# A two-layer memory-augmented transformer on one core: P times V as one 128-row product per head, V in 64-column tiles, and a new order of TensorE's work

## The chip, the cores and the metric

The kernel runs on one core of one Trainium2 chip. Its time is the device time of one execution in microseconds (us). Three runs of the kernel before took 2775.19, 2775.85 and 2778.07 us, so the median is 2775.85 us. The profile below is of one more execution, whose span is 2772.4 us.

## What is computed

The input has 2048 rows of width 576. Attention (A) and a gated feed-forward net (B) follow each other, and the pair is applied twice with the same weights:

```python
x = x + A(layernorm(x));  x = x + B(layernorm(x))
x = x + A(layernorm(x));  x = x + B(layernorm(x))

# A: 64 segments of 32 rows, one after the other; 32 heads of 128
for s in range(64):
    h = concat([mem, xs[s]])                 # 8 memory rows + 32 rows = 40 tokens
    q, k, v = h @ Wq, h @ Wk, h @ Wv         # 576 -> 32 x 128 each
    p = softmax(mask(q @ k.T * 128**-0.5))   # 40 x 40 for each head
    o = (p @ v) @ Wo                         # 32 x 128 -> 576
    mem, out[s] = o[:8], o[8:]               # the next segment reads mem
# B: out = (silu(x @ w1) * (x @ w3)) @ w2, inner width 4608
```

A segment needs the memory rows that the segment before it made, so each layer is a chain of 64 steps. The kernel runs the two layers together: step t works on segment t of the first layer and on segment t-7 of the second (a lag of seven). There are 71 steps, t = 0 to 70. In steps 7 to 64 two segments go through every product together, as 80 columns ("double steps", 58 of them); the first seven and the last six steps have one segment, 40 columns ("single steps").

## The kernel before

576 is four chunks of 128 and a remainder of 64. Each product is therefore a node of 128-row matmuls and a small node for the remainder of 64 rows, with two remainders side by side in the upper and the lower half of the array. The program is made of such nodes. Each node of TensorE has a letter and a tiling of the array, which the planner calls its mode:

| letter | node | tile (rows x columns) |
|---|---|---|
| Q, q | Q and K of four heads; remainder | 128x128; 64x128 |
| S | scores | 128x64 |
| T, P | transpose of the probabilities; P times V | 128x128; 64x128 |
| O, o | output product; remainder | 128x128; 128x64 |
| X, x | V of segment rows; remainder | 128x32; 64x32 |
| V, v | V of memory rows (and the segment rows next to them); remainder | 128x32; 64x32 |
| F, f, W | feed-forward up, its remainder, down | 128x128; 64x128; 128x128 |
| m, a, b, p, n | small transposes | 128x128 |

The planner takes the order of these nodes from a string, `ORDER = FIRST + FOUR * 11 + LAST`; FOUR is a stretch of four steps that stands eleven times. From it, and from model times, it assigns copies out of PSUM to ScalarE or VectorE ("AD" nodes). The parts that the change touches:

```python
def v_nodes(name, t, prio, tail_at, emit, users, deps, tail_deps):
    sl = Slot("v", users=users)              # one of 4 buffers of V
    b = banks()                              # two PSUM banks
    m_ = node("PE", ..., mode="c32", acq=[sl] + b, name=name)
    n = node("PE", ..., deps=[m_] + tail_deps, mode="oct", name=name + "t")
    ev = [node("AD", ew(512), em.v_ev(sl, r, b[r]), deps=[n], ...) for r in (0, 1)]

def v_mm(self, t, b, strips, tail):          # four strips of 32 columns
    for c in ((4,) if tail else range(4)):
        for r in (0, 1):
            for p0, c0, q in strips:
                out = self.bk(b[r])[p0:p0 + 32, :]
                ...                          # HTt[:, c, c0:c0+32] x W[:, c, 512 columns]

def v_ev(self, v, r, b):
    return lambda n: self.cp(n, self.T.V[:, v.i, r, :], self.bk(b)[:])

def pv(self, t, g, pts, vx, vm, b):          # eight heads
    todo = [(0, s) for s in vx] + [(1, vm)]
    for hl in range(4):
        for m, s in todo:
            for ab in (0, 1):
                rr = slice(ab * R64, (ab + 1) * R64)
                self.mm(bank[ab][...], self.T.V[rr, s.i, ...], PT[rr, m, hl, :],
                        m == todo[0][0], m == 1, tile_position=(ab * R64, 0))

def step(t):
    for k in ((0, 1) if e else (0,)):        # e = role(t): 1 in even steps
        ... v_nodes("VM", ...)
    for g in range(NG):                      # four groups of eight heads
        ...                                  # Q q Q q, S, softmax, T, copies to PTS, P, copies to OT, O, o

def load_qk(self, kind):                     # all of Wq, then all of Wk, then both remainders
    for c in range(4):
        self.dma(self.T.W[:, 4 * kind + c, :], wd[c * P:(c + 1) * P, :])
    if kind:
        for r, wd in ((0, self.a.wq), (1, self.a.wk)):
            self.dma(self.T.W[r * R64:(r + 1) * R64, 8, :], wd[4 * P:D, :])   # 64 partitions
```

In the last function the remainder of Wq lies in partitions 0 to 63 and that of Wk in 64 to 127. The remainder of Wv is loaded as two such halves. The pool `pts` has one buffer: a T has to wait until the P before it has read it.

Of the kernel before, what the change touches and what calls it, by code (L numbers as in the profile page):

```python
# [13 lines left out]
P = 128  # L14
R64 = 64
# [16 lines left out]
SWITCH = 0.1  # L32
# [3 lines left out]
POOLS = {"bank": 7, "y": 1, "qkt": 4, "v": 4, "sme": 2, "pb": 2, "pts": 1, "ot": 2,  # L36
         "xr": 4, "xn": 2, "w13": 2, "w2": 2, "htt": 4}
# [7 lines left out]
class Slot:  # L45


    def __init__(self, pool, users=1):
        self.pool, self.users, self.i, self.end = pool, users, None, 0.0


class Node:
# [11 lines left out]
    def after(self, *more):  # L64
        for d in more:
# [7 lines left out]
         "WO": "O", "WOt": "o", "VX": "X", "VXt": "x", "VM": "V", "VMt": "v", "FF": "F", "FFt": "f", "W2": "W"}  # L73


def plan(nodes, pools, letters):
# [24 lines left out]
    def est(e, n):  # L101
        t = max(t_eng[e], n.ready)
        need = {}
        for s in n.acq:
            need[s.pool] = need.get(s.pool, 0) + 1
        for p, c in need.items():
            t = max(t, sorted(free[p])[c - 1])
        return t
# [4 lines left out]
    while len(order) < len(nodes):  # L113
# [32 lines left out]
        for s in n.acq:  # L146
            f = free[s.pool]
            s.i = min((i for i in range(len(f)) if f[i] <= st + 1e-9), key=lambda i: f[i])
            f[s.i] = NOW
# [32 lines left out]
def ewh(*ns):  # L182
# [5 lines left out]
    "maQQqqSQQqQQqSQqqTqSQVvVqPvTOPSToOPXOToPoxOoQQqqQQSqqQSqVQqvQSTqPQTqPSTOoPOOToPoaOoQQqqQQqqSVSvQQqqQTSqQqPVSTOPv"  # L188
    "oTXPOToPOOooxQQqqQQSqqQqSQQqVSqQqvTSPTOPoTOPoTOPoOoQQpqqVQvqSQnQqqFQqfSTFfPSQQqqWFTOPfSoFOfVvTWFPfoXTFPOOoofxQqQ"
    "QqqQFSqfVSvQWQqqQTqSQPqFfOTFfPSoTWPOFofOTFPfoOoWQQqqFQfqVvWFQqfSFQSfqVvWQFqfQSqTFfPQOTqWFPfSoTFPfOOWToPoOoabQQqq"  # L190
    "QQqqSVSvQQqqXxTSXxPQTQqqOSPToPOOToPoOoQQpqqQQSqqQQqqSVVvvTnQPqSFTQPfqOFSofXTOoPxWTFFfPfOOooWQQqqFfQFSfqQQqqVSvQT"
    "QqqFQPfSqFWSfXTFfPxOTOWooPFTFffPOOooWQFqfQqQFafqQWFSqfQQqqSFWQqfVVSvvFfTQqPWFSfTFfPOToWPOoTOPoOboQQqqQpQSqqQXxSQ"
    "qqVSvQqTQPqXTSPxOTOoPoTPOOoonQQpqqQQSqqVnQqSvQQqqFTfFPfQOTqSoFWVvSfPFTWOPfXTOFxofPFOWooWQfqQQqqQFfqSVvWFWQTqfSQX"
    "xqFWQqPfSWQTOqPFoSfOTFPfoWFTWOPfFOooWQfqQQqQqqSWQFfqSVvFTQqWQqfWaQqPFSSfTFVvfPOWWFTfoOPoTWPOOoobQQqqQQSqqQQSqqVX"
    "TvSxQqPQTqOoSPXxTOPopTWPOOoon"
)
FOUR = (
    "QQqqQpQSqqVVvvQTQqqPSnQFQSqqfOTFPfSoXxTFfPFWWOFToffPOOooWWFQfqQQqqQFqfSFWWQfqXVxvSQTWQqqFPfSTWQFPfqOOToSoWFPfFTO"
    "PfWOooFQfqQQqqWWFQqfVSSvQQqqWFTQqfPSWFQfqVvSTWWFFPffOoTOPoTWPOoOoabWQQqqQQSqqQQqqVSSvXxTQqPQqTOPSXxoTOPopTOPoOon"
)  # L200
LAST = (
    "QQqqQpQqqSVvSQnQqqQTqQFqPfSSFTOPfVvFTOoofPFWWTOPfoFOfoWQWFqfQQqqWFWQSfqVXxvQSqXxQqTFQqPfSQFfqOTFWPfoSWOTFfPFTOoo"
    "fPWOWoFQqfFWWQqfFQSfqQVvqQWQSqqWTFQfqQSPqWFTOSoPfVWFvfTOPoTWPOOoobQqpQQqqQSqQqSXVvxQTqQSPqQTqXPSOxoOTWPToPOOoonQ"
    "QqqpQSqVQnvqQTSqPFQfqFQTOqfPSFQOqfVoSovWWTFfPFTOPfWOFWooXxQqfVQqvQQSqqWQqSFTQqfFWQQqSqPfTFSPfOWTOooWPFTFfPfOOooW"
    "WQFfqQqFQQqfqSWFWQqfSVvFQfqWWSFQqfTFfPQqWTWOFSoPfVvTOWoPTWPOObooQQpqqQQSqqQQqqSnXVvxFfSTQqPQFTqfOoSPFTOoPfWTOPFO"
    "fooFQqfQqVSQvQqqWQTFfqFSPfVQqvWTQFSfqFQPqfOOoSoWTFfPXxTFPfWOOooFQfqQqQQSqqQSVqvWQTFfqQSPqFfQqTOSoPWOTFPfoTFfPOOo"
    "oWQqFQfqQQSqqVvSQQqqQTQqqSPTSVPFvOToOPoTfOoPOopWnFFffFfFWfFFffWFfWFfFfFWfFfFWfFFffWFfFfWFfFfWW"
# [4 lines left out]
class Opt:  # L212

    qk, qkt, sc, tr, pv, wo, wog, vm = 0.0079, -0.0342, 0.0268, 0.1447, 0.0406, 0.2653, 0.0725, 0.1407
    vmt, vx, vxt, ff, fft, win, w2, gstep = -0.0231, 0.2313, 0.0843, 0.2124, -0.1839, 2.4, 0.1943, 0.0624
# [3 lines left out]
def make_nodes(em, nseg, pools, o=Opt, dma_bw=230e3, load_bw=380e3):  # L219
# [26 lines left out]
    ld_m0 = load("m0", kb(8, D), -10, em.load_m0())  # L246
    ld_qk = [load("ldqk", kb(576, 4096), kd - 9.0, em.load_qk(kd)) for kd in (0, 1)]
    ld_v = [load("ldv", kb(576, 4096), -7.0, em.load_v())]
# [44 lines left out]
    vx_slots, vx_nodes, vx_pe, last_v = {}, {}, [None], [None]  # L293

    def v_nodes(name, t, prio, tail_at, emit, users, deps, tail_deps):
        sl = Slot("v", users=users)
        b = banks()
        m_ = node("PE", 8 * 0.2165, emit(b, False), deps=deps, prio=prio, mode="c32", acq=[sl] + b, name=name)
        n = node("PE", 0.2165, emit(b, True), deps=[m_] + tail_deps, prio=prio + tail_at, mode="oct", name=name + "t")
        reads_ht.setdefault(t, []).extend([m_, n])  # L300
        ev = [node("AD", ew(512), em.v_ev(sl, r, b[r]), deps=[n], prio=prio, rel=[b[r]], name=name + "e") for r in (0, 1)]
        return sl, ev, n

    def vx_pair(t, prio):

        deps = [ht_ready[li, s] for s in (t, t + 1) for li in layers_of(s) if s == t or li]
        for k in ((0, 1) if both(t) else (0,)):
            sl, ev, vx_pe[0] = v_nodes("VX", t, prio + 0.01 * k, o.vxt, (lambda k: lambda b, tail: em.vx(t, k, b, tail))(k), 4,
                                       deps + vx_pe + last_v, [])
            for kk in ((k,) if both(t) else (0, 1)):  # L310
                vx_slots[t, kk], vx_nodes[t, kk] = sl, ev

    def step(t):
# [9 lines left out]
        vm_slots, vm_nodes = {}, {}  # L323
        for k in ((0, 1) if e else (0,)):
            pv_ = t + o.vm + 0.01 * k
            sl, ev, last_v[0] = v_nodes("VM", t, pv_, o.vmt, (lambda k: lambda b, tail: em.vm(t, k, b, tail))(k), 2 if e else 4,
                                     hm[:1] + hx + (ld_v if t == 0 else []), hm[1:])
            for kk in ((k,) if e else (0, 1)):
                vm_slots[kk], vm_nodes[kk] = sl, ev
        me = steps[t]  # L330
        if t == nst - 1:
            last_reads[0].append(last_v[0])
        y = Slot("y", users=2)
        wos, wots = [], []
        for g in range(NG):
            k = g // 2
            qs, qe = [], []
            for u in (2 * g, 2 * g + 1):
# [3 lines left out]
                m_ = node("PE", 32 * mm80, em.qk(t, u, b), deps=hx + hm[:1] + (ld_qk if t == 0 else []),  # L342
                          prio=pq, mode="full", acq=[q] + b, name="QK")
                n = node("PE", 4 * mm80, em.qk_tail(t, u, b), deps=[m_] + hm[1:], prio=pq + o.qkt, mode="row", name="QKt")
                rd += [m_, n]
                me[f"QK{u}"], me[f"QKt{u}"] = m_, n
                for kind in (0, 1):
                    qe.append(node("AD", ew(256, 64) if nl == 2 else ew(160), em.qk_ev(t, u, kind, q, b[kind]), deps=[n], prio=t + o.ustep * u,
                                   rel=[b[kind]], name="QKe"))
# [10 lines left out]
            w = 0.168 * (4 if nl == 2 else 2 - e) + nl * 320 / 960  # L360
# [8 lines left out]
            x_slots = [] if nl == 1 and e else [vx_slots[t - e, k]]  # L369
            x_nodes = [] if nl == 1 and e else vx_nodes[t - e, k]  # L370
            pv = node("PE", (8 if x_slots else 4) * mm80, em.pv(t, g, pts, x_slots, vm_slots[k], b), deps=pe_ + vm_nodes[k] + x_nodes,
                      prio=pf + o.pv, mode="row", acq=b + [ot], rel=[pts, vm_slots[k]] + x_slots, name="PV")
# [11 lines left out]
        if t == nst - 1:  # L384
            last_reads[1].extend(me[f"QKt{u}"] for u in range(8))
# [21 lines left out]
    last_up = [None]  # L407
# [3 lines left out]
    def job(j):  # L411
# [10 lines left out]
        prev_ff = last_up[0]  # L422
        cost = ewh(640)
        for (bi, g) in reversed(ents):
            pa = post(bi, g)
            wr += ln_nodes("F", xr[g], Slot("xn"), [pa], s0, [((lambda bi: lambda b: em.xtb_write(bi, b))(bi), cost, [prev_ff])], last)
# [14 lines left out]
        for at, pp in enumerate([npp - 1] + list(range(npp - 1)) if last else range(npp)):  # L441
            mids, w2s, htts, lds = [], [], [], []
            stays = last and pp == npp - 1
            for pr_ in (2 * pp, 2 * pp + 1):
# [8 lines left out]
                else:  # L453
                    keep = s0 < nst <= s0 + 4 and pp == npp - 1
                    w13, w2 = Slot("w13", users=1 + keep), Slot("w2", users=ne + keep)
# [8 lines left out]
                          acq=b + [htt], name="FF")  # L464
                ff = node("PE", 2 * mm, em.ffn_up(ents, pr_, w13, b, last and not stays, True), deps=[fm], prio=prio + o.fft, mode="row",
                          rel=rel13, name="FFt")
                a = node("ACT", actc(256 * ne), em.ffn_tanh(ents, b, htt), deps=[ff], prio=prio - 0.5, name="tanh")
                c = node("DVE", 2 * dve(256 * ne) + 0.13, em.ffn_mul(ents, b, htt), deps=[a], prio=prio - 0.5, rel=b, name="mul")
                last_up[0] = ff
                mids.append(c)  # L470
                htts.append(htt)
            for (bi, g) in ents:
                b = banks()
                d = node("PE", 8 * 0.1225, em.ffn_down(bi, pp, htts, w2s, b, last and not stays), deps=mids + lds, prio=prio + o.w2,
                         mode="full", acq=b, rel=htts + w2s, name="W2")
# [11 lines left out]
    def x_in(g):  # L487
        xn = Slot("xn")
        ld = node("DMA", 0.8, em.load_xn(g, xn), deps=reads_ht.get(4 * g - 3, [])[:1], prio=4 * g - 3.0 if g else -11, acq=[xn],
# [12 lines left out]
    for t in range(nst):  # L502
# [4 lines left out]
        if role(t) == 0:  # L507
            vx_pair(t, t - 1 + o.vx)
# [19 lines left out]
class Emitter:  # L528
# [28 lines left out]

    def swdma(self, out, in_):
        self.ch("POOL", self.nc.gpsimd.dma_start(out=out, in_=in_))
# [6 lines left out]


# [27 lines left out]
    def load_m0(self):  # L595
        return lambda n: self.dma(self.T.M0[0:MEM, :], self.a.mem0[0])

    def load_qk(self, kind):
        def f(n):
            wd = (self.a.wq, self.a.wk)[kind]  # L600
            for c in range(4):
                self.dma(self.T.W[:, 4 * kind + c, :], wd[c * P:(c + 1) * P, :])
            if kind:
# [628 lines left out]
```

## Time and profile before

| | busy, us | share of the span |
|---|---|---|
| TensorE matmuls (PE) | 2723.5 | 98% |
| TensorE weight loads (PEld) | 2252.7 | 81% |
| VectorE (DVE) | 2047.1 | 74% |
| ScalarE (ACT) | 1091.0 | 39% |
| GpSimd (POOL) | 328.4 | 12% |

A record of a matmul covers its whole way through the array, some 180 to 200 ns for 80 columns, while matmuls of one kind start every 36 ns. Busy time of PE therefore overlaps itself, and the distance from one start to the next tells more. The trace has 60919 matmuls. Every one of them can be assigned to its letter, since the number of matmuls of each node is fixed by the code.

### The profile page before, as it was taken

What the parts mean: (1) busy time and instruction counts of PE and PEld (TensorE: products, weight loads), DVE (VectorE), ACT (ScalarE), POOL (GpSimd) and SP (SyncE); (2) the same over time, 40 slices, a digit from 0 to 9 for tenths busy, and PEclk for the clock granted to TensorE, in tenths of its full rate; (3) what the DMA queues carried; (4) which work ended last, traced back from release to release, by engine and by line L of the source; (5) the groups of instructions that cost most, each with busy time, mean ns of one, the idle gap of its engine ahead of it and who ended that gap; (6) DMA issues with size and microseconds to landing.
All of it is one profiled execution on the core that took longest, in us unless ns stands there. A gap on an engine that the chain in (4) does not pass through costs nothing.

```text
span 2772.4 us, 136269 instructions
## 1 busy us (share of the span) xinstructions
PE 2723.5 (98%) x60919; PEld 2252.7 (81%) x60919; DVE 2047.1 (74%) x5584; ACT 1091.0 (39%) x3339; POOL 328.4 (12%) x399
## 2 busy tenths in 40 slices
PE   5999999999999999999999999999999999999999
PEld 4887888888888888888888888888888888878887
DVE  4677777777777777777777777777777777687776
ACT  1434343433434343343434334343433434343332
POOL 1111010110101011010101101010101101010110
PEclk9999999999999999999999999999999999999999
DMA  8062614244242424424152342415234241523467
GB/s 308 13 198 69 184 53 138 81 121 124 78 131 62 140 82 116 128 78 131 56 146 82 112 133 77 131 49 153 82 106 138 73 130 57 142 79 107 141 182 235
DMA packets 481691, 322.02 MB, mean 116 GB/s; under 512 B 26216, under 2 KB 476656, under 8 KB 479440
## 3 DMA queue, kind: packets, MB, share of 16 engines
q1 hardware_dynamic: 478080, 306.38, 37.7%
q8 instruction: 476, 7.80, 1.2%
q0 software_dynamic: 3024, 6.93, 0.9%
q14 instruction: 111, 0.91, 0.1%
HBM read 308.49 MB, written 2.36 MB: 112 GB/s over the span
## 4 chain that ended last, share of the span: by engine, by line
PE 96%; DMA 2%; ACT 1%; DVE 1%; issue 0%; SPq 0%; ACTq 0%; DVEq 0%
PE bank L547 82%; PE YB L547 14%; DMA W<-in_A_Wk_dram 1%; DMA W<-in_B_w_dram 1%; DMA WV<-in_B_w_dram 0%; SPq L556 0%; DMA W<-in_A_Wq_dram 0%; ACT OT L550 0%; DVE STAT L553 0%; ACT HT L550 0%; DVE SME L553 0%; ACT PTS L550 0%; DVE PB L553 0%; DVE PTS L553 0%; ACT QKT L550 0%
## 5 line engine op out<-in xcount | busy, mean ns | idle before, releaser
L547 PEld LDWEIGHTS <-W 128*128 128x128 bf16 (+1 forms) x29080 | 1231.6, 98 | 144.4 <-issue 37.7
L547 PE MATMUL bank<-HT,W 128*128 128x80 bf16 (+3 forms) x22720 | 816.4, 198 | 23.1 <-DMA W<-in_A_Wk_dram 12.1
L547 PE MATMUL bank<-XTB,W 128*128 128x256 bf16 (+1 forms) x6360 | 658.2, 261 | 1.6 <-ACT XTB L550 0.8
L906 POOL MEMSET PB<- 128x1024 bf16 x284 | 270.0, 951 | 2065.9 <-PE bank L547 1626.9
L550 ACT ACTIVATE QKT<-bank 128x64 bf16<-128x64 f32 (+1 forms) x1348 | 312.6, 315 | 445.0 <-PE bank L547 434.4
L547 PE MATMUL YB<-OT,WO 128*128 128x80 bf16 (+3 forms) x11360 | 429.2, 199 | 5.0 <-ACT OT L550 3.9
L547 PEld LDWEIGHTS <-WO 128*128 128x128 bf16 (+1 forms) x11360 | 385.2, 102 | 36.0 <-issue 17.4
L547 PE MATMUL bank<-WV,HT 128*32 128x512 bf16 (+1 forms) x6840 | 380.8, 382 | 0.0
L553 DVE CAST QKT<-bank 128x64 bf16<-128x64 f32 (+1 forms) x716 | 193.6, 316 | 243.5 <-PE bank L547 242.3
L547 PE MATMUL bank<-W2C,HTT 128*128 128x288 bf16 x2240 | 312.5, 287 | 0.2 <-issue 0.2
L553 DVE TENSOR_REDUCE STAT<-SME 104x8 f32<-104x320 f32 (+1 forms) x568 | 271.5, 478 | 44.8 <-ACT SME L550 41.2
L553 DVE TENSOR_TENSOR PB<-SME,STAT 40x128 bf16<-40x128 f32 (+1 forms) x1004 | 283.7, 321 | 12.9 <-DVE STAT L553 0.5
L547 PEld LDWEIGHTS <-HT 128*32 128x32 bf16 (+1 forms) x6840 | 150.2, 95 | 173.4 <-issue 48.1
L547 PEld LDWEIGHTS <-HTT 128*128 128x128 bf16 x2304 | 211.5, 98 | 57.4 <-issue 4.9
L553 DVE SCALAR_TENSOR_TENSOR XR<-bank,XR 128x288 f32<-128x288 f32 x576 | 241.2, 447 | 10.6 <-PE bank L547 4.6
L550 ACT ACTIVATE HTT<-bank 128x512 bf16<-128x512 f32 (+1 forms) x324 | 175.0, 549 | 182.8 <-PE bank L547 182.6
L550 ACT ACTIVATE SME<-SME 104x320 f32<-104x320 f32 (+1 forms) x284 | 133.4, 470 | 262.0 <-DVE SME L553 261.6
L553 DVE SCALAR_TENSOR_TENSOR HTT<-HTT,bank 128x512 bf16<-128x512 bf16 (+1 forms) x324 | 201.5, 622 | 41.2 <-ACT HTT L550 39.1
L550 ACT ACTIVATE PTS<-bank 128x320 bf16<-128x320 f32 (+1 forms) x386 | 146.5, 411 | 206.1 <-PE bank L547 143.0
L550 ACT ACTIVATE OT<-bank 128x320 bf16<-128x320 f32 (+1 forms) x358 | 141.1, 413 | 212.4 <-PE bank L547 212.0
L553 DVE TENSOR_TENSOR HTT<-HTT,bank 128x512 bf16<-128x512 bf16 (+1 forms) x324 | 203.6, 628 | 24.2
L550 ACT ACTIVATE V<-bank 128x512 bf16<-128x512 f32 x269 | 147.2, 596 | 173.9 <-PE bank L547 173.4
(64 smaller groups left out, 1676.3 us busy)
## 6 DMA issues: line engine op xcount, KB each, us to landing
W<-in_B_w_dram SPq DMA_DIRECT2D x612, 256.0 KB, 3.8
W2C<-in_B_w_dram SPq DMA_DIRECT2D x306, 288.0 KB, 3.2
W<-in_B_w_dram SPq DMA_DIRECT2D x612, 32.0 KB, 3.3
W<-in_B_w_dram SPq DMA_DIRECT2D x10, 512.0 KB, 8.2
WO<-in_A_Wo_dram SPq DMA_DIRECT2D x4, 1152.0 KB, 17.2
XR<-in_A_x_dram POOLq DMA_DIRECT2D x16, 288.0 KB, 3.1
W<-in_A_Wq_dram SPq DMA_DIRECT2D x4, 1024.0 KB, 8.4
W<-in_A_Wk_dram SPq DMA_DIRECT2D x4, 1024.0 KB, 15.0
```

The lines of the kernel that those rows point to most:

```text
L547: self.ch("PE", self.nc.tensor.matmul(out, lhsT=lhsT, rhs=rhs, start=start, stop=stop, skip_group_check=True, **k))
L550: self.ch("ACT", self.nc.scalar.activation(*a, **k))
L553: self.ch("DVE", getattr(self.nc.vector, fn_)(*a, **k))
L906: return lambda n: self.ch("POOL", self.nc.gpsimd.memset(self.T.PB[:, pb.i], 0.0))
```

## The change

It makes one tile of V for all heads, with the segment rows' V in partitions 0 to 63 and the memory rows' V in 64 to 127, so that P times V is one product over 128 rows for each head. V's own product is laid out in two 64-column tiles in double steps where two segments' rows lie side by side (the nodes X of double steps, and V of even double steps); the other V nodes keep 32-column tiles. Copies of V out of PSUM follow the heads and rows, as pieces of 64 or 32 partitions. A remainder may now stand ahead of its main product (`begin` sets the start flag on whichever comes first), and the remainders of Wq, Wk and Wv are loaded as 128-partition transfers. Wq and Wk come in two halves of heads, the first x and mem0 go by ScalarE's queue, OT has four buffers and XR three. The order strings are new, the lag is still seven. FIRST and LAST are cut below.

```diff
-SWITCH = 0.1
+SWITCH = 0.098
-POOLS = {"bank": 7, "y": 1, "qkt": 4, "v": 4, "sme": 2, "pb": 2, "pts": 1, "ot": 2,
-         "xr": 4, "xn": 2, "w13": 2, "w2": 2, "htt": 4}
+POOLS = {"bank": 7, "y": 1, "qkt": 4, "sme": 2, "pb": 2, "pts": 1, "ot": 4,
+         "xr": 3, "xn": 2, "w13": 2, "w2": 2, "htt": 4}
 ...   (FIRST and LAST: other strings, cut; w is a W of the second layer)
 FOUR = (
-    "QQqqQpQSqqVVvvQTQqqPSnQFQSqqfOTFPfSoXxTFfPFWWOFToffPOOooWWFQfqQQqqQFqfSFWWQfqXVxvSQTWQqqFPfSTWQFPfqOOToSoWFPfFTO"
-    "PfWOooFQfqQQqqWWFQqfVSSvQQqqWFTQqfPSWFQfqVvSTWWFFPffOoTOPoTWPOoOoabWQQqqQQSqqQQqqVSSvXxTQqPQqTOPSXxoTOPopTOPoOon"
+    "QQqqQpQqqSVSVvvnQQqqQQqqSTFPFffXSxTOPWwTFPFTffOPOOWwFfooooFQfqQQqqFWQfqSXSxQQqqwFQfqVvTQFPqfSFWfSTOwPFTFPffOTOPW"
+    "OoooowQFfqFQfqWQQqqSVSvwQQqqFTQSfqWFwQqfFPfSVvTWwPFfTOPaTWOPOOoooobwQQqqQQSqqQQSqqVvTSXxQQqPQqTOPSoTXxpOPoTPOOoon"
 )
 ...
+        modes = ("col", "quad") if strips[0][3] == R64 else ("c32", "oct")
+        m_ = node("PE", 8 * 0.2158, emit(b, False), deps=deps, prio=prio, mode=modes[0], acq=b, name=name)
+        n = node("PE", 0.2158, emit(b, True), deps=deps + tail_deps, prio=prio + tail_at, mode=modes[1], acq=b, name=name + "t")
+        for r in (0, 1):
+            outs = em.v_parts(strips, r)
+            for p0, width, row, blk in outs:
+                e = node("AD", ew(512), em.v_ev(b[r], p0, width, row, blk), deps=[m_, n] + free.get(blk % 4, []), ...)
 ...
-        for k in ((0, 1) if e else (0,)):
+        for k in ((0, 1) if e and both(t) else (0,)):
 ...
-            pv = node("PE", (8 if x_slots else 4) * mm80, em.pv(t, g, pts, x_slots, vm_slots[k], b), ..., mode="row", ...)
+            pv = node("PE", 8 * mm80, em.pv(t, g, pts, b), deps=pe_ + vx_ev["VM", t, g] + vx_ev["VX", t - e, g], mode="full", ...)
 ...
+    def wide(self, k, c0, row):
+        return [(R64 * ab, c0, 2 * k + ab, R64, row) for ab in (0, 1)]
+    def narrow(self, c0, row):
+        return [(64 * ab + 32 * i, c0, 2 * i + ab, 32, row) for ab in (0, 1) for i in (0, 1)]
 ...
-            for hl in range(4):
-                for m, s in todo:
-                    for ab in (0, 1):
-                        rr = slice(ab * R64, (ab + 1) * R64)
-                        self.mm(self.bk(b[ab])[...], self.T.V[rr, s.i, g % 2, hl * E:(hl + 1) * E], PT[rr, m, hl, :],
-                                m == todo[0][0], m == 1, tile_position=(ab * R64, 0))
+            for j in range(GH):
+                self.mm(self.bk(b[j // 4])[...], self.T.V[:, self.head(g, j) // 4, ...], self.T.PTS[:, pts.i, j * nq:(j + 1) * nq], True, True)
 ...
+    def load_qkt(self):
+        for kind, wd in ((0, self.a.wq), (1, self.a.wk)):
+            self.dma(self.T.W[:, 8, kind * 2048:(kind + 1) * 2048], wd[4 * P:D, :].rearrange("p (r n) -> r p n", r=2))
+    def load_vt(self):
+        return lambda n: self.dma(self.wv(True), self.a.wv[4 * P:D, :].rearrange("p (r n) -> r p n", r=2))
```

## The prediction

> **What bounds the kernel now.** I read the busy shares first, then the chain that ended last, then what TensorE waited for, and only then single groups.
>
> ```profile
> PE 2723.5 (98%) x60919; PEld 2252.7 (81%) x60919; DVE 2047.1 (74%) x5584; ACT 1091.0 (39%) x3339; POOL 328.4 (12%) x399
> PE 96%; DMA 2%; ACT 1%; DVE 1%; issue 0%; SPq 0%; ACTq 0%; DVEq 0%
> ```
>
> TensorE (PE) is on 96% of the chain, and no other engine is near full. Its waits, first in the first 80 us, then from 80 to 2680 us:
>
> ```profile
> PE bank L547 <- DMA W<-in_A_Wk_dram: 12.1, 5, 3.0
> PE bank L547 <- DVE XN L553: 5.1, 1, 5.1
> ...
> PE YB L547 <- ACT OT L550: 3.5, 14, 0.3
> PE bank L547 <- ACT HT L550: 3.2, 7, 0.7
> PE bank L547 <- ACT PTS L550: 1.5, 5, 0.4
> ```
>
> The figures after a name are total us, times, and the longest. Behind the start TensorE waits under 10 us in 2600. So the time is the sum of TensorE's own stream, plus a start that waits for weights. I take the stream apart by the distance from one matmul's start to the next in the trace.
>
> Within a node, starts stand at the pace of the columns: 36.0 ns for 80 columns, 25 for 40, 56 for 128, 109 for 256, 123 for 288, about 216 for a set of 512-column tiles that run side by side. Multiplied by the counts in the code, with pairs and sets counted once, that is 2454.9 us.
>
> Where two neighbouring nodes have **different tilings**, there is a gap on top: 134 ns from the last 80-column start of a full node to the first of a 64-row node (medians over 520 cases), where 36 would be the pace. Walking the order string with the tile table gives 2137 such boundaries, and the trace has exactly 2137. Their mean excess is 0.1008 us, so they cost 215.4 us.
>
> The stream runs from 4.8 to 2768.2 us. 2763.4 - 2454.9 - 215.4 leaves 93 us: 38 before the first Q of step 1 (at 60.4 us), about 8 after the last step's first Q, and the rest small, about 0.6 us a double step. A FOUR block takes 162.2 us; its stream is 148.4 and its 114 boundaries 11.5, so 2.3 us are anything else. The model is tight enough to price a change.
>
> **What the Trainium skill says.** "TensorEngine Tiling (Array Packing)", Key Properties: changing the tiling mode, not just the tile, drains TensorE. The trace agrees, with the 0.1008 us above. "TensorE: Matmul & The Clock Gate", Part 3, The mechanism: tiles at different positions start about 4 ns apart and run together. The trace agrees: 4 ns within a pair of P or a set of V. So two 64-column tiles should stream V as fast as four 32-column ones. "SBUF — State Buffer", Door 1: 64 partitions reach 8 of 16 DMA ports, 218 against 436 GB/s at best. The trace agrees: 415 GB/s from 14 to 24 us, 236 while the 64-partition remainders of Wq and Wk land (24 to 30), 250 in the stretch of Wv's (38 to 43). "TensorEngine Tiling", PSUM Bottleneck: tiling speeds TensorE up and not the copies out of PSUM. That bears on V's copies below.
>
> **The change part by part.**
>
> *Boundaries.* P becomes a full node like its neighbours T and O; wide V shares the 128x64 tiling with S and o. Walking the new strings with the new tiles I count 1779 boundaries: 423, 11 x 94 and 322 in FIRST, FOUR and LAST, against 508, 11 x 114 and 375. Boundaries that touch a P fall from 379 to 127. 358 x 0.1008 = **-36.1 us**, all on TensorE's path.
>
> *Stream.*
>
> ```profile
> L547 PE MATMUL bank<-WV,HT 128*32 128x512 bf16 x5472 | 322.9, 381 | 0.0
> L547 PE MATMUL bank<-PTS,V 64*128 64x80 bf16 x3712 | 107.0, 199 | 1.5 <-ACT PTS L550 0.8 <-DVE PTS L553 0.5
> ```
>
> The columns are shape, count, busy us and mean ns, idle before. P goes from 16 half-height matmuls in 8 pairs (36.6 ns a pair) to 8 of 36 ns: nothing gained in streaming, though the count halves. In seven even single steps P had only its memory half, 4 pairs at 25 ns; eight full ones add 4 x 25 ns x 28 groups = +2.8 us. V nodes fall from 171 to 165 (seven second nodes go, one X comes), each nine sets of 0.2158 us: -11.7 us. In double steps V keeps its time. Together **-8.9 us**.
>
> *Start.* The same 18.9 MB of weights must land before step 0 can end; by the DMA rates the last WO is there near 53.7 us, and step 1 starts at 60.4. Full-width remainders save about 2.6 us (1.42 MB in 24 to 30 us, at 415 GB/s it is 3.4) and 2.0 us (1.25 MB in 38 to 43). The weights' first issue moves up from 1.6 to 0.8 us. With half the heads' Wq and Wk there by about 15 us, Q starts 10 us earlier, so little is left when WO lands: I take 3 of the 6.7 us behind it as saved. I call it **-8.5 us**, an estimate.
>
> *V's copies.*
>
> ```profile
> L550 ACT ACTIVATE V<-bank 128x512 bf16<-128x512 f32 x269 | 147.2, 596 | 173.9 <-PE bank L547 173.4
> L553 DVE CAST V<-bank 128x512 bf16<-128x512 f32 x73 | 50.2, 689 | 39.6 <-PE bank L547 37.1
> L553 DVE TENSOR_REDUCE STAT<-SME 104x8 f32<-104x320 f32 x464 | 222.7, 480 | 37.6 <-ACT SME L550 34.8
> L553 DVE TENSOR_REDUCE STAT<-SME 40x8 f32<-40x320 f32 x104 | 48.8, 469 | 7.2 <-ACT SME L550 6.5
> ```
>
> Each bank was one copy, 342 in all. Now a wide node has 4 (116 nodes) and a narrow one 8 (49 nodes): 856. The last two lines show that fewer partitions don't shorten an instruction (469 against 480 ns), so a piece costs what the whole did: 514 x 0.6 = 308 us more on ScalarE and VectorE together, which take 3138 of 2 x 2772 now. They go from 57% to about 62%, and VectorE gives back some 18 us (one P-probability instruction fewer in 116 groups). That fits beside TensorE, but the two banks of a narrow node are held about 2.5 us with both engines copying, before under 1. I put +3 us on it.
>
> *New waits in the order.* T directly followed by its own P leaves nothing to cover the copy to PTS. The old order has that once, the new one 18 times (once in each FOUR). T's last matmul takes 202 ns, the copy 437 to 490, with semaphores some 0.7 us: 17 x 0.7 = **+12 us**. P to O is covered better in return (filler under 0.6 us in 12 places of steps 8 to 63 before, 2 after): -3, which cancels the +3 above.
>
> Although a remainder may go first, none does: pairing the letters, no q, f, x or v precedes its main node. The permission itself is worth nothing.
>
> Sum: 2775.85 - 36.1 - 8.9 - 8.5 + 12 + 3 - 3 = 2734.35, say **2734 us**, 1.5% less.
>
> **Rivals.**
>
> *Copies become the bound.* If banks come back late, TensorE stalls at the Q after a V node. For it: 2.5 times as many copies, seven banks, narrow nodes in every odd step. Against it: ScalarE is idle 61% of the time, and the order was laid out with these copies in it. At 0.5 us for each of 100 V nodes the gain shrinks by 50 and the time is near 2780; at 0.1 us it is 2742.
>
> *The drains are worth more than I count, or the waits less.* If T-P pairs wait 0.3 us instead of 0.7, and step 1 starts by 48 us, the time is near 2723; with V in fewer, wider matmuls also shedding a few ns a set, 2715.
>
> *The start is hidden anyway.* Step 0 also runs through softmax and the copies; if step 1 still starts near 60 us, 8 us are missing: 2743.
>
> **Range and chances.** The boundary term is counted, and priced by 2137 cases; I give it 3 us either way. The start is open by 5, the T-P waits by 5, the copies by -3 to +25. That makes 2712 to 2760 for eight in ten. Faster by over 2% means below 2720.3, which takes the good side of two terms: 0.2. Slower by over 2% means above 2831, which only a broken overlap of V's copies would give: 0.03.
>
> **What would show it.** Boundaries: 56311 matmuls (2048 fewer for P, 2560 fewer for V) in the trace, 128-row P at 36 ns, 1779 gaps of about 0.1 us. Start: Q of step 1 near 52 us, and no stretch near 240 GB/s in the first 45. Copies: 856 of V, about 0.6 us each, ScalarE near 50%. Waits: PE on PTS rising from 2 us to some 12, in 18 places. A FOUR block should take 162.2 - 2.0 + 0.7 = 160.9 us. I am wrong if that block is above 162, which would mean waits for PSUM banks that I can't see in the string; they would appear as PE waiting for V's copies, or as idle before Q.

## The result and the profile after

The changed kernel takes 2794.32 us (median of four runs, 2793.55 to 2795.23) against 2775.58 us: 1.0066 times as long, 95% interval 1.0052 to 1.008. The prediction was 2734 us. Its profile has a span of 2791.7 us. The busy shares and the chain that ended last:

```profile
PE 2696.5 (97%) x56311; PEld 2278.6 (82%) x56311; DVE 2161.8 (77%) x5663; ACT 1297.0 (46%) x3693; POOL 328.0 (12%) x399
PE 83%; ACT 6%; DVE 5%; issue 3%; DMA 2%; SPq 1%; POOL 1%; DVEq 0%; POOLq 0%; ACTq 0%
```

TensorE's work shrank: 56311 matmuls, as counted, and 27 us less busy time. But its share of the chain fell from 96% to 83%, and ScalarE and VectorE hold 11% of it. TensorE's own stream no longer sets the time alone. TensorE's three longest waits in the first 80 us (total us, times, longest):

```profile
PE bank L551 <- DMA W<-in_A_Wk_dram: 20.2, 8, 12.4
PE bank L551 <- DMA WV<-in_A_Wv_dram: 10.1, 1, 10.1
PE bank L551 <- DMA W<-in_A_Wq_dram: 8.6, 2, 7.5
```

And in the eleven FOUR blocks, before (one line) and after:

```profile
PE YB L547 <- ACT OT L550: 2.8, 11, 0.3
...
PE bank L551 <- ACT PTS L554: 4.9, 11, 0.4
PE bank L551 <- DVE PB L557: 3.4, 11, 0.3
PE bank L551 <- DVE HTT L557: 3.0, 11, 0.6
PE bank L551 <- ACT V L554: 2.0, 11, 0.2
```

Each stands there eleven times, once a block. PTS holds the transposed probabilities that P reads, PB the probabilities that T transposes, HTT the feed-forward's hidden values that W reads, and the wait for V is for a PSUM bank that a copy of V has not yet left. Assigning the matmuls to their letters as before gives the stretches, each from the first start of its first node:

| stretch | before, us | after, us | expected change | measured |
|---|---|---|---|---|
| to the first Q of step 1 | 60.4 | 85.5 | -8.5 | +25.1 |
| steps 1 to 15 | 489.4 | 485.5 | -9.8 | -3.9 |
| eleven FOURs | 1784.5 | 1782.8 | -14.5 | -1.7 |
| LAST, to the last matmul's start | 433.8 | 433.4 | -8.6 | -0.5 |

The fourth column splits the prediction's boundaries, stream and T-P terms by where their letters stand; together it is the predicted gain of 41 us. The misses are 34, 6, 13 and 8 us. The start is over half of it, and something that lies in every stretch is the rest. For the start the DMA view from 16 to 22 us:

```profile
DMA packets 76, 0.31 MB, mean 52 GB/s; under 512 B 0, under 2 KB 0, under 8 KB 76
q1 hardware_dynamic: 76, 0.31, 12.6%
```

In 6 us 76 packets of 4 KB moved, each 159 ns: 76 x 0.159 / 6 = 2.0 engines at work, and 12.6% of sixteen is the same two. This is the remainder of Wq, the new 128-partition transfer, and nothing else moves beside it.

For the rest, the groups of P and of V's copies (shape, count, busy us and mean ns, idle before them):

```profile
L551 PE MATMUL bank<-PTS,V 128*128 128x80 bf16 x1856 | 110.1, 201 | 7.7 <-ACT PTS L554 5.7 <-DVE PTS L557 1.4
L554 ACT ACTIVATE V<-bank 64x512 bf16<-64x512 f32 x329 | 186.5, 588 | 107.4 <-PE bank L551 103.8
L554 ACT ACTIVATE V<-bank 32x512 bf16<-32x512 f32 x255 | 144.8, 585 | 50.4 <-PE bank L551 47.2
L557 DVE CAST V<-bank 32x512 bf16<-32x512 f32 x137 | 94.1, 687 | 30.7 <-PE bank L551 26.3 <-ACT V L554 1.2
```

A copy of 32 or 64 partitions takes the 0.59 or 0.69 us that a whole bank took. Count and price are as predicted. What they do to TensorE was not, and one place in a block's timeline shows how (start, length, instruction, idle before it):

```profile
1364.05 4.48 ACT L554 ACTIVATE V<-bank 32x512 bf16<-32x512 f32 x8
...
1367.14 0.64 PE L551 MATMUL bank<-PTS,V 128*128 128x80 bf16 x8
...
1367.96 1.60 PE L551 MATMUL bank<-HT,W 128*128 128x80 bf16 x40 [0.18 <-ACT V L554]
```

ScalarE is 46% busy over the whole, and for these 4.5 us it does nothing but copies of V. P loses 0.19 us in its middle, and then Q loses 0.34 waiting for a bank that still holds V, together 0.53 us behind the pace.

### The profile page after: what moved, and what is told of

Its sections match the earlier page's. It is cut to its first block, busy times and chain, and to the rows that moved or that the text cites. A ratio compares the mean times of both kernels' runs of the same rounds, so it can differ in the third digit from the quotient of the medians.

```text
span 2791.7 us, 127415 instructions
## 1 busy us (share of the span) xinstructions
PE 2696.5 (97%) x56311; PEld 2278.6 (82%) x56311; DVE 2161.8 (77%) x5663; ACT 1297.0 (46%) x3693; POOL 328.0 (12%) x399
## 4 chain that ended last, share of the span: by engine, by line
PE 83%; ACT 6%; DVE 5%; issue 3%; DMA 2%; SPq 1%; POOL 1%; DVEq 0%; POOLq 0%; ACTq 0%
PE bank L551 73%; PE YB L551 10%; ACT V L554 4%; DVE HTT L557 1%; SPq L560 1%; DMA WV<-in_A_Wv_dram 1%; DVE STAT L557 1%; DVE PB L557 1%; ACT PTS L554 1%; DMA W2C<-in_B_w_dram 1%; DMA W<-in_A_Wk_dram 1%; DVE XN L557 1%; ACT OT L554 0%; POOL PB L949 0%; DVE V L557 0%
## 5 line engine op out<-in xcount | busy, mean ns | idle before, releaser
L554 ACT ACTIVATE QKT<-bank 128x256 bf16<-128x256 f32 (+2 forms) x1304 | 300.5, 311 | 340.5 <-PE bank L551 339.0
L551 PE MATMUL YB<-OT,WO 128*128 128x80 bf16 (+3 forms) x11360 | 407.5, 199 | 4.2 <-issue 3.4
L554 ACT ACTIVATE V<-bank 64x512 bf16<-64x512 f32 (+1 forms) x584 | 331.3, 587 | 157.8 <-PE bank L551 150.9
L551 PEld LDWEIGHTS <-WO 128*128 128x128 bf16 (+1 forms) x11360 | 375.5, 102 | 22.6 <-issue 14.4
L551 PE MATMUL bank<-WV,HT 128*64 128x512 bf16 (+3 forms) x4280 | 380.7, 387 | 10.7 <-DMA WV<-in_A_Wv_dram 10.1
L557 DVE CAST QKT<-bank 128x256 bf16<-128x256 f32 (+1 forms) x760 | 205.2, 317 | 188.9 <-PE bank L551 185.7
L551 PEld LDWEIGHTS <-HT 128*64 128x64 bf16 (+3 forms) x4280 | 180.4, 103 | 141.2 <-issue 58.4
L557 DVE TENSOR_TENSOR PB<-SME,STAT 40x192 bf16<-40x192 f32 (+4 forms) x916 | 276.7, 336 | 11.9
L554 ACT ACTIVATE OT<-bank 128x320 bf16<-128x320 f32 (+1 forms) x451 | 169.4, 411 | 167.4 <-PE bank L551 163.6
L557 DVE CAST V<-bank 64x512 bf16<-64x512 f32 (+1 forms) x272 | 186.9, 687 | 36.3 <-PE bank L551 28.5
```

The lines of the kernel that those rows point to most:

```text
L551: self.ch("PE", self.nc.tensor.matmul(out, lhsT=lhsT, rhs=rhs, start=start, stop=stop, skip_group_check=True, **k))
L554: self.ch("ACT", self.nc.scalar.activation(*a, **k))
L557: self.ch("DVE", getattr(self.nc.vector, fn_)(*a, **k))
```

## The experiments

The first theory, **engines**: the remainders' transfers run on two DMA engines, and that is the start's loss. Its rival, **halves**: the start is late because Wq and Wk now come in halves of heads, in 2 KB packets. For the other stretches, **copies**: late copies of V, and what they delay, eat the saved boundaries. Its rival, **order**: the short distances in the new string do.

All runs from the fourth row on are the run with 64-partition remainders (the third row) with something more changed, and are compared with it. Step 1's start and the FOUR block (median of eleven) come from the traces; a time of one run stands in brackets.

| run | step 1, us | FOUR, us | time, us | against before |
|---|---|---|---|---|
| before | 60.4 | 162.21 | 2774 to 2776 | |
| the change | 85.5 | 162.00 | 2794.32 | 1.0066 (1.0052 to 1.008) |
| 64-partition remainders | 63.1 | 161.97 | 2769.73 | 0.9983 (0.9976 to 0.999) |
| short copies | 61.2 | 160.34 | 2741.38 | 0.9879 (0.9865 to 0.9894) |
| short 32-partition copies | 60.5 | 161.20 | (2755.07) | |
| old FOUR | 60.9 | 168.23 | 2835.57 | 1.0216 (1.0199 to 1.0233) |
| V in 32-column tiles | 61.5 | 162.84 | (2776.22) | |
| P in halves | 62.4 | 163.57 | (2801.06) | |
| planner's times true | 61.5 | 164.09 | 2794.41 | 1.0069 (1.0052 to 1.0085) |
| two queues | 63.1 | 162.00 | 2769.21 | 0.9974 (0.9964 to 0.9985) |
| Wv's remainder first | 61.6 | 161.99 | 2768.31 | 0.9973 (0.9963 to 0.9983) |
| O between T and P | 61.0 | 161.60 | (2766.16) | |
| all three together | 62.4 | 161.61 | 2763.15 | 0.9961 (0.9947 to 0.9975) |

### Remainders as two transfers of 64 partitions

```diff
-    self.dma(self.T.W[:, 8, kind * 2048:(kind + 1) * 2048], wd[4 * P:D, :].rearrange("p (r n) -> r p n", r=2))
+    for r in (0, 1):
+        self.dma(self.T.W[r * R64:(r + 1) * R64, 8, kind * 2048:(kind + 1) * 2048], wd[4 * P:D, r * 2048:(r + 1) * 2048])
```

(The same for Wv's.) Expected:

> The changed kernel, with each remainder of Wq, Wk and Wv loaded as two transfers of 64 partitions, to the same places. Theory: the lost time is the start; the three remainder transfers of 128 partitions move at about 52 GB/s (some 13 packets of 4 KB a us, 159 ns each, so two DMA engines at work), since their outer dimension is 2; then step 1 starts near 54 us in place of 85.5 and the kernel takes 2763 us (2760 to 2767). Rival: the start is late because Wq and Wk come in halves of heads, in 2 KB packets, ahead of everything else; then step 1 stays above 80 us and the time above 2789.

Step 1 starts at 63.1 us, 22.4 earlier, and the time falls by 25 to 2769.73 us, under the kernel before. The halves of heads are still there, so "engines" holds, and "halves" is not what cost these 22 us. TensorE's waits for weights, as above, and the DMA view from 14 to 20 us, while the same remainders of Wq and Wk are landing:

```profile
PE bank L551 <- DMA W<-in_A_Wk_dram: 10.0, 8, 2.3
PE bank L551 <- DMA W<-in_A_Wq_dram: 2.6, 1, 2.6
PE bank L551 <- DMA WV<-in_A_Wv_dram: 1.6, 3, 1.0
...
DMA packets 505, 1.39 MB, mean 232 GB/s; under 512 B 73, under 2 KB 73, under 8 KB 505
```

That is 232 GB/s against 52. The Trainium skill states this: "DMA: Bandwidth & Descriptors", section "Why a DMA increments its semaphore by 16 and not by 1", says that the number of engines is the largest up to 16 that divides the slowest dimension of both access patterns. `r p n` put a 2 there; the two engines above agree, though no run varies that 2 alone. But the gain was 22 us where 31 was expected: step 1 starts no earlier than before the change. By 30 us this run has moved 9.27 MB and the kernel before 10.20, so its weights are still later; whether the halves of heads have a part in that, no run tells.

### Short copies of V

```diff
-    self.cp(n, self.T.V[row:row + width, blk, :], self.bk(b)[p0:p0 + width, :])
+    self.cp(n, self.T.V[row:row + width, blk, 0:32], self.bk(b)[p0:p0 + width, 0:32])
```

This leaves 480 of 512 columns of V out; count, order and semaphores stay.

> As the run with 64-partition remainders, and each copy of V out of PSUM takes 32 of its 512 columns (the rest of V keeps old values, so P times V is left incomplete); same instructions, order and waits. Theory: of the 4.2 us by which a FOUR block exceeds stream and boundaries, some 1.4 are late copies of V and what they delay on ScalarE and VectorE; the block falls from 162.05 to about 160.6 us and the kernel to some 2740. Rival: the new order's own short distances (T to P) make the waits; then the block stays above 161.6 and the kernel within 8 us of the run with 64-partition remainders.

A copy now takes 0.19 us. The block falls by 1.63 us, and the kernel by 28. TensorE's waits in the eleven blocks are then:

```profile
PE bank L551 <- ACT PTS L554: 4.8, 11, 0.4
PE bank L551 <- DVE PB L557: 0.3, 1, 0.3
PE bank L551 <- DVE HTT L557: 0.2, 1, 0.2
```

Compared with the four lines after the change, the wait for V's bank is gone, and those for PB and HTT are all but gone. These two are VectorE's work, and not of V at all: they stood late because the copies took ScalarE's and VectorE's time ahead of them. The wait for PTS, the T-P place, stays. So the length of the copies costs 28 us, about as much as was missed outside the start (27 us), and "copies" accounts for it; "order" has the one wait left. The run shortens all 856 copies, also the share of their work that the kernel before had, so for the change's extra copies alone 28 us is rather an upper figure.

### Only the 32-partition copies short

```diff
-    self.cp(n, self.T.V[row:row + width, blk, :], self.bk(b)[p0:p0 + width, :])
+    self.cp(n, self.T.V[row:row + width, blk, 0:32 if width == 32 else 512],
+            self.bk(b)[p0:p0 + width, 0:32 if width == 32 else 512])
```

> As the run with 64-partition remainders, with only the 32-partition copies of V shortened to 32 columns (V is left incomplete there); the 64-partition ones are whole. Shortening all of them took the block from 161.97 to 160.34 us. If the eight pieces of an odd step, which stood in ScalarE's queue for 4.5 us on end, are the trouble, the block falls to 160.9 or less; if the 64-partition copies of even steps delay the feed-forward's and softmax's work, it stays above 161.3. I expect both, near 161.1.

Here 480 of 512 columns are left out of the 32-partition copies alone. The block falls from 161.97 to 161.20, which is 0.77 of the 1.63 us. Two of its waits, with their lines in the eleven blocks:

```profile
PE bank L551 <- DVE HTT L557: 3.1, 11, 0.6
...
PE bank L551 <- DVE PB L557: 0.3, 1, 0.3
```

The 0.53 us at P and Q above are down to 0.05, and PB's wait is all but gone. HTT's 0.41 in the middle of a block stays: that one belongs to the 64-partition copies. In the block both kinds share the cost about evenly.

### The old FOUR under the new tilings

```diff
-FOUR = "QQqqQpQqqSVSVvvnQQqqQQqqSTFPFffXSxTOPWwTFPFTff..."
+FOUR = "QQqqQpQSqqVVvvQTQqqPSnQFQSqqfOTFPfSoXxTFfPFWwO..."   # the string of before, each second W a w
```

> As the run with 64-partition remainders, with the FOUR string of the kernel before under the new tilings (each second W is a w). By count 109 boundaries a block instead of 94 (before: 114). If the copies of V cost nothing in this order, the block is 148.4 + 109 x 0.1008 + 2.3 = 161.7 us, 0.35 less than the new order's 162.05; if the copies disturb an order that was not laid out for them, over 163. So: 0.1 to 0.5 us a block for the theory that the new order's waits eat its saved boundaries, and 1 us or more above for the rival that the new order was needed for the copies.

The block takes 168.23 us, over 6 us more, so the second guess was right: with these copies the new order saves far more waiting than its own short distances cost. TensorE's waits in these blocks:

```profile
PE bank L551 <- ACT V L554: 19.8, 22, 0.9
PE bank L551 <- ACT PTS L554: 13.5, 33, 0.7
PE bank L551 <- DVE PB L557: 12.7, 11, 1.2
PE bank L551 <- DVE V L557: 6.4, 11, 0.6
```

They come to 4.8 us a block, against 1.2 in the base, and the 15 more boundaries are 1.5. The planner has shared out the copies anew for this order, which is part of what was compared.

### V in 32-column tiles, and P in halves

Two runs undo one tiling each and keep the copies. V:

```diff
+    strips = [(p0 + x, c0 + x, q, 32, row) for p0, c0, q, m, row in strips for x in range(0, m, 32)]
```

> As the run with 64-partition remainders, with each 64-column tile of V split into two of 32 columns side by side; copies, order and everything else as they are. By count 104 boundaries a FOUR block instead of 94, 1919 in all instead of 1779. If boundaries are worth their 0.1008 us here, the block takes 163.05 us and the kernel 14 us more than with 64-column tiles; if waits absorb them, less than 0.4 us a block.

P, with the 64-row products in the form of before (they sum other halves than attention does):

```diff
-    for j in range(GH):
-        self.mm(bank[j // 4][...], self.T.V[:, h // 4, ...], self.T.PTS[:, pts.i, j * nq:(j + 1) * nq], True, True)
+    for hl in range(4):
+        for m in (0, 1):                     # j = hl + 4 * m
+            for ab in (0, 1):                # rr = the half ab of the rows
+                self.mm(bank[ab][...], self.T.V[rr, h // 4, ...], self.T.PTS[rr, pts.i, ...], m == 0, m == 1, tile_position=(ab * R64, 0))
```

> As the run with 64-partition remainders, with P again as 16 products of 64 rows in pairs, of the form of the kernel before (the pairs add up other halves than the reference's, so the output is not attention's). By count 116 boundaries a FOUR block instead of 94, 2154 in all instead of 1779. If the tiling boundaries of P are worth their price under the late copies too, the block takes 162.0 + 2.2 = 164.2 us and the kernel 30 to 38 us more; if the waits would have filled the same time anyway, under 1 us a block. The 64-column split gained 0.87 a block of its counted 1.0, so I expect 1.8 to 2.2.

V's 10 boundaries a block are worth 0.87 us (1.01 by count), P's 22 are worth 1.60 (2.22), under the 1.8 to 2.2 expected. At most places of P in that trace the excess is the 0.1 us of the count. The sum is less because TensorE then arrives later at places where it would wait anyway: with V in 32 columns the wait for HTT falls from 0.40 to 0.29 us a block; with P in halves it is gone, and the waits for PB and PTS fall by 0.12 and 0.10. Over the whole kernel, against the base's median, V's single run is 6.5 us longer where the count says 14, and P's 31 us where it says 38. Start and LAST differ by up to 2.6 and 5 us between runs with the same code there, so the block is the better measure.

### The planner's times set to the measured ones

```diff
-    e = node("AD", ew(512), em.v_ev(...), ...)
+    e = node("AD", (0.589, 0.685), em.v_ev(...), ...)
```

> As the run with 64-partition remainders, with the planner's time for a copy of V set to what the trace shows (589 ns on ScalarE, 685 on VectorE) instead of 494 and 598; TensorE's order is the same, and the copies are shared out anew. If the waits come from copies that take longer than the plan thought, and so stand in the wrong queue, the block falls by 0.5 to 1.2 us of the 1.63 that short copies gave, and the kernel to some 2755. If it is the sheer work of the copies, the block stays within 0.3 us of 161.97.

Both guesses fell. The block takes 164.09 us, 2.1 more. The copies are shared out anew, which moves other work too, and in the blocks TensorE now waits for PB:

```profile
PE bank L551 <- DVE PB L557: 23.6, 22, 2.0
```

So a truer time for one kind of copy, with the order kept, made the plan worse. Whether an order searched anew with these times would do better was not tried.

### The start, and T next to P

Two runs took up the start, one the place between the last T of a block and the end of its P, where 0.61 + 0.18 us are lost. (The string in the change's diff has one Q too many here; the kernel's own end is below.)

```diff
-    self.dma(self.T.W[r * R64:(r + 1) * R64, 8, ...], ...)                      # first run: two queues
+    (self.adma if r else self.dma)(self.T.W[r * R64:(r + 1) * R64, 8, ...], ...)
-    load("ldvt", kb(64, 4096), -6.5, em.load_vt())                              # second: Wv's remainder first
+    load("ldvt", kb(64, 4096), -7.5, em.load_vt())
-    "...XxQqPQqTOPSoTXxpOPoTPOOoon"                                            # third: O between T and P
+    "...XxQqPQqTOPSoTXxpOPoTOPoOon"
```

> As the run with 64-partition remainders, with the upper halves of the two remainders of Wq and Wk issued from ScalarE's queue, so that both halves of the partitions are written at one time. If the rate of those 64-partition transfers (some 246 GB/s from 14 to 20 us) is what is left of the start's loss, about 2.5 us are gained: step 1 near 60.5 us, the kernel near 2767. If V's product and its 16 copies set the end of step 0, nothing is gained beyond 1 us.

> As the run with 64-partition remainders, with the remainder of Wv loaded ahead of Wv's four chunks instead of behind them. In the run before, that remainder shared the DMA engines with WO from 40 to 48 us, and V's remainder products, then 16 copies, P and WO followed; step 1 started at 63.1 us. If the arrival of the last of Wv sets the end of step 0, it comes some 4 us earlier and step 1 starts near 59, the kernel takes about 2766. If the arrival of WO sets it, step 1 stays at 61 to 63 and the time within 1.5 us.

> As the run with 64-partition remainders, with the end of FOUR changed from o T P O O o o n to o T O P o O o n, so that an output product lies between the last T and its P. That takes away the 0.62 + 0.18 us seen at this place in each block, and adds two tiling boundaries (0.2 us), and P then has 0.34 us to its own O instead of 1.2. If the short distance from T to P costs what the trace shows, the block falls by 0.2 to 0.5 us from 161.97; if another late copy stands behind it, the block is unchanged or longer.

The second queue changed nothing in the start (63.1 us). Wv's remainder first gave 1.5 us (61.6), where 4 were expected; runs with the same loads spread from 60.5 to 63.1, so this is no clear gain. It fits the guess that WO's arrival sets step 1, though TensorE shows no wait for WO in this run. The third took 0.37 us from the block, as expected. Together:

> The changed kernel with what the runs pointed to: 64-partition remainders with the upper halves of Wq's and Wk's on ScalarE's queue, Wv's remainder ahead of Wv, and the end of FOUR with an output product between the last T and its P. A block takes 161.6 us and step 1 starts at 60 to 62 us; from 2769.7 us, 0.37 x 11 = 4 us for the order and 0 to 2 for the start: 2764 to 2766 us. If the start's pieces add up after all, 2761.

2763.15 us, 0.9961 of the kernel before (0.9947 to 0.9975): the fastest that computes everything. Of the 6.6 us under the base, 4 are the order's; step 1 starts at 62.4 us, so the start's pieces did not add up.

## Why the prediction was wrong

**Start: the step that failed most.** I priced the remainders from "full-width", that is from how many partitions they write, and took 4.6 us for it. The trace has those transfers at 52 GB/s, two engines. The outer dimension of 2 was in the diff that I quoted. With it mended, 22.4 of the 34 us come back. The second part of the term was wrong too: I let WO's arrival, near 53.7 us, set the end of step 0, and had WO come sooner. WO's last transfer lands at 56.5 us before the change, at 60.5 with 64-partition remainders and at 59.4 with Wv's remainder first. In the changed kernel and in these two runs TensorE does not wait for it: from the last wait for Wv to step 1 it is 14.4 us after the change (71.1 to 85.5), 15.1 with 64-partition remainders (48.0 to 63.1) and 15.1 with Wv's remainder first (46.5 to 61.6), with V's products, the copies, and P and O in turn. An earlier Q gives nothing there. But WO follows closely: with 64-partition remainders it lands 1.0 us before its last product starts at 61.55, and in the run with V in 32-column tiles TensorE does wait for it:

```profile
PE YB L551 <- DMA WO<-in_A_Wo_dram: 0.6, 2, 0.3
```

So what is left of the start's miss is that the weights come later than I said; why they do was not settled by these runs.

**Boundaries: right.** 1779 gaps are in the trace, their medians are as before (134 ns from a full to a 64-row node; before the change 299 of these end on 80 columns, and the 520 I gave count all of them). In the block, undoing them costs 86% and 72% of the count. The stream term too: without the copies' length a block takes 160.34 us where 160.9 was said.

**V's copies: the term that was mis-sized.** I counted 856 and priced them at 0.6 us, both right, and then put +3 us on their effect, because the mean load of two engines rose only to 62%. The runs show up to 28. The mean was the wrong view: eight copies stand together in one queue for 4.5 us while VectorE is in the softmax, and what comes late is PB and HTT as well as V. I had named late copies as a rival, and 8 us was its mild case. The 28 lie between its two cases. The rival had the right cause, but looked for it only at the Q behind a V node; PB and HTT, 6.4 of the 8.4 us of waits that the copies brought to the eleven blocks, it did not name.

**T-P waits: right in kind, too large.** PTS keeps TensorE waiting 10.1 us between 80 and 2680 us where it was 2.1 before, so 8 us more, where the sum had +12. An O in between gave 0.37 us a block. The P-to-O relief is not shown to be the order's: the 2.8 us of waits for OT are gone, but they are gone under the old FOUR as well, and OT now has four buffers.

With short copies the kernel takes 2741 us, its step 1 starting 9 us later than I said, and 2734 + 9 is 2743. That this is so close is in part luck: the sum still holds 3 us for the copies, the eleven blocks gained 5 us more than said (19.5 for 14.5) and LAST 5 less (3.7 for 8.6).

## What to carry to other kernels

A count of tiling boundaries in TensorE's order, times the gap that the trace shows, predicted well here, but only while the copies out of PSUM keep up; ask for each burst of copies which queue takes it, for how long, and what else waits in that queue, since a mean load of 46% did not show it. Read every DMA's access pattern for its outermost dimension before counting partitions: a 2 there cost this kernel 22 us. The old order cost 6 us a block under the new copies, so a change of tiling and its order belong together in one estimate.

## What was not expected of the hardware

A 512 KB load written as `[2, 64, 2048]` on the source side moved at 52 GB/s with two engines. With each such load split into two of 64 partitions the DMA moved 232 GB/s while they landed; that one load wrote all 128 partitions was no help.
